# K's transform in an S4 convolution mixed with a gated unit: split as 64 by 32 points instead of 32 by 64

## The chip, the cores and the metric

The kernel runs on one core of one Trainium2 chip. The metric is the device time of one execution in microseconds, the median of several runs.

## The reference

From u (2048 x 512) the reference computes a long convolution `a` and a gated unit `b` and mixes them by a gate `g` for each row:

```
P = exp(dt * A * l)                       # 512 channels, 128 states, 2048 steps
K = einsum("dn,dnl,dn->dl", C, P, dB).real    # the kernel K, one row of 2048 for each channel
a = irfft(rfft(pad(u)) * rfft(pad(K)))[:2048] + u * Dskip
b = (sigmoid(u @ w_gate) * (u @ w_up)) @ w_down     # 512 -> 1792 -> 512
g = sigmoid(sum(u * gate_w))
out = g * a + (1 - g) * b
```

## The kernel before

All data are fp32. The three products of the gated unit use a split of every operand into two fp32r parts and three matmuls; the convolution uses plain fp32 matmuls, of which each call shows as two MATMUL rows in the trace.

**The gated unit** runs in two halves of 1024 rows, each in two blocks of 512 rows and 14 blocks of 128 hidden columns in groups of 3, 4, 4 and 3. `hidden` (L871) makes `gups` (L894), `post` makes sigmoid times up and splits it (L911 to L918), `down` makes `dps` (L946), and `add` adds it to `acc` (L962, L966). The split weights are written to DRAM (`wsp`) in the first half and read back in the second.

**The convolution** is a transform of 2048 points with a frequency shifted by a quarter, split in two stages. Of u, 64 points go first: `rows` (L531) makes `ups` (L556) for each of 16 row tiles and stores it to `a_u`. Of K, 16 groups of 32 channels are built one after the other: `preludes`, `bases` and `tables` make exponentials and sines on ScalarE and tables T (32 powers of the 64-step) and B (64 powers of the step) on VectorE; 64 calls in tiles of 128 rows by 32 columns multiply them to `kps` (L476), which `first` (L485) evicts to `kst`: a channel's 2048 values lie as 32 partitions by 64. `first` then does K's first stage: 32 points across the partitions, for two channels at a time with a block-diagonal weight `wk`, 32 calls in 64x64 tiles with 64 columns, into two banks `wps` (L503). Four evictions (L515) put them in `kev`, and every second group goes to DRAM (`a_k`, L519).

**`passes`** (L585) runs when u is done and a half of the channels (256 wide, `WIDTHS`) has its K. For each half j it takes eight steps p. A step loads u's second-stage weights `wwu` (L601) and two pieces of `a_u` (`au`, L606), and for r = 0, 1 K's second-stage weights `wwk` (L615, 128 KB each) and a piece of `a_k` (`ak`, L618), then the inverse weights `wwv` (L622). `ustep` makes `s2u`: 16 calls in 64x32 tiles, 256 columns (L639), and evicts it to `uf`. `kstep` runs once for each r: four calls in 128x64 tiles, 256 columns, into one bank `s2k` (L664), and on VectorE two products with `uf` (L673, L674) and two sums (L679, L680) for the complex product. `inverse` makes `ips` (L700) in four banks, evicts it to `ev` (L709) and stores it to `b_s`. `finals` and `last` read `b_s` back (`b_in`, L736), make `fps` (L748) and mix it into `acc` or `al`.

**Order.** The kernel is straight-line code. A planner (`Plan`, L128) takes the strands (generators) above and emits, at each moment, the step whose start plus a bias is smallest, by costs written beside each step; `BIAS`, `CHANGE`, `PACE`, `SLACK` and `EARLY` (L51 to L60) are its constants. It holds buffer slots (`slots`) and PSUM banks: three for `gups`, one for `dps` (both for `dps` at the end), and four, `XB`, for all the convolution's matmuls. All loads and stores go out in one order on SyncE's queue. K's products, sums and all the gated unit's elementwise work share VectorE and ScalarE.

## Time and profile before

| | |
|---|---|
| median of 3 runs | 648.77 us (648.64 to 650.41) |
| the profiled execution | 648.06 us, span 646.3 us |
| busy, share of the span | TensorE 98%, VectorE 86%, ScalarE 58% |
| granted TensorE clock | 1.000 |
| DMA | 133.93 MB, 207 GB/s over the span |

The profile counts time from the first instruction. "PE" is a matmul and "PEld" a weight load; a matmul's end is modelled, so its row includes a latency after the last column. A row of a group gives count, busy time and mean duration of one, then the idle time before it and what ended it. "SPq" rows are issues of transfers on SyncE's queue.

### The profile page before, as it was taken

What the parts mean: (1) busy time and instruction counts of PE and PEld (TensorE: products, weight loads), DVE (VectorE), ACT (ScalarE), POOL (GpSimd) and SP (SyncE); (2) the same over time, 40 slices, a digit from 0 to 9 for tenths busy, and PEclk for the clock granted to TensorE, in tenths of its full rate; (3) what the DMA queues carried; (4) which work ended last, traced back from release to release, by engine and by line L of the source; (5) the groups of instructions that cost most, each with busy time, mean ns of one, the idle gap of its engine ahead of it and who ended that gap; (6) DMA issues with size and microseconds to landing.
All of it is one profiled execution on the core that took longest, in us unless ns stands there. A gap on an engine that the chain in (4) does not pass through costs nothing.

```text
span 646.3 us, 15757 instructions
## 1 busy us (share of the span) xinstructions
PE 631.1 (98%) x6560; PEld 468.3 (72%) x6560; DVE 555.8 (86%) x953; ACT 374.3 (58%) x584; POOL 0.2 (0%) x4
## 2 busy tenths in 40 slices
PE   4999999999999999999999999999999999999996
PEld 3777777777787778877766787867787776666664
DVE  6859999999999999999999999999999836546515
ACT  5788787857677666576566857564676221333210
POOL 0000000000000000000000000000000000000000
PEclk9999999999999999999999999999999999999999
DMA  7974763745574446569158674542195688798377
GB/s 225 385 243 176 235 195 102 285 143 199 200 294 131 180 164 227 178 236 349 29 186 261 222 263 150 177 132 74 38 337 185 213 268 261 203 301 244 86 247 265
DMA packets 79622, 133.93 MB, mean 207 GB/s; under 512 B 7104, under 2 KB 53056, under 8 KB 74944
## 3 DMA queue, kind: packets, MB, share of 16 engines
q1 hardware_dynamic: 79552, 132.94, 62.5%
q8 instruction: 51, 0.84, 0.5%
q14 instruction: 19, 0.16, 0.1%
HBM read 79.43 MB, written 53.48 MB: 206 GB/s over the span
## 4 chain that ended last, share of the span: by engine, by line
PE 78%; DVE 14%; ACT 3%; issue 2%; DMA 1%; DVEq 0%; SPq 0%
PE gups L894 39%; PE dps L946 20%; PE kps L476 5%; PE s2k L664 4%; PE wps L503 2%; PE ips L700 2%; PE ups L556 2%; PE s2u L639 2%; PE fps L748 2%; DVE T L424 1%; DVE T L423 1%; DVE ex L395 1%; DVE t L422 1%; DVE sg L913 1%; DVE acc L966 1%
## 5 line engine op out<-in xcount | busy, mean ns | idle before, releaser
L894 PE MATMUL gups<-x,gu 128*128 128x512 f32 x1344 | 329.9, 395 | 9.2 <-ACT x L815 6.4
L894 PEld LDWEIGHTS gups<-x,gu 128*128 128x128 f32 x1344 | 251.6, 189 | 74.7 <-issue 10.0
L946 PE MATMUL dps<-dnw,h 128*128 128x512 f32 x672 | 177.5, 400 | 0.5 <-DVE h L918 0.2
L946 PEld LDWEIGHTS dps<-dnw,h 128*128 128x128 f32 x672 | 121.6, 188 | 42.7 <-issue 12.0
L917 ACT ACTIVATE h<-sg 128x512 fp32r<-128x512 f32 x56 | 35.1, 628 | 76.6 <-DVE sg L913 76.3
L673 DVE TENSOR_TENSOR tt<-s2k,uf 128x512 f32<-128x512 f32 x32 | 22.0, 688 | 31.7 <-PE s2k L664 30.7
L913 DVE TENSOR_TENSOR sg<-gups,sg 128x512 f32<-128x512 f32 x56 | 38.4, 686 | 11.5 <-PE gups L894 6.1
L515 ACT ACTIVATE kev<-wps 128x256 f32<-128x256 f32 x64 | 33.1, 672 | 25.3 <-PE wps L503 25.3
L422 DVE TENSOR_TENSOR t<-T,bz 128x64 f32<-128x64 f32 (+4 forms) x80 | 46.0, 575 | 1.0
L424 DVE TENSOR_TENSOR T<-T,t 128x64 f32<-128x64 f32 (+4 forms) x80 | 46.2, 577 | 0.7
L423 DVE TENSOR_TENSOR T<-T,bz 128x64 f32<-128x64 f32 (+4 forms) x80 | 46.0, 575 | 0.0
L966 DVE SCALAR_TENSOR_TENSOR acc<-dps,omg,acc 128x512 f32<-128x512 f32 x48 | 35.8, 747 | 10.4 <-PE dps L946 10.2
L918 DVE TENSOR_TENSOR h<-sg,h 128x512 fp32r<-128x512 f32 x56 | 38.5, 687 | 5.1 <-ACT h L917 4.9
L709 ACT ACTIVATE ev<-ips 128x256 f32<-128x256 f32 x64 | 19.8, 388 | 35.6 <-PE ips L700 32.8
L911 ACT ACTIVATE sg<-gups 128x512 f32<-128x512 f32 x56 | 33.5, 599 | 8.1 <-PE gups L894 7.9
L451 DVE TENSOR_TENSOR B<-ep 128x1024 f32<-128x1024 f32 x32 | 37.9, 1218 | 0.0
L476 PEld LDWEIGHTS kps<-B,T 128*32 128x32 f32 x2048 | 29.6, 110 | 6.8 <-issue 4.0
L394 ACT ACTIVATE af<-ex 128x1216 int32<-128x1216 f32 x16 | 19.6, 1222 | 25.3 <-DVE ex L385 25.3
L476 PE MATMUL kps<-B,T 128*32 128x64 f32 x2048 | 32.2, 220 | 0.6 <-DVE T L424 0.2
L664 PE MATMUL s2k<-ak,wwk 128*64 128x256 f32 x256 | 31.4, 386 | 0.0
L911 ACT ACT_TABLE_LOAD x23 | 29.5, 1283 | 0.4
L398 ACT ACTIVATE af<-ex 128x1216 f32<-128x1216 f32 x16 | 19.6, 1225 | 17.3 <-DVE ex L395 17.3
(79 smaller groups left out, 657.7 us busy)
## 6 DMA issues: line engine op xcount, KB each, us to landing
wsp<-gu SPq DMA_DIRECT2D x14, 1024.0 KB, 4.8
gu<-wsp SPq DMA_DIRECT2D x14, 1024.0 KB, 5.2
a_u<-evu SPq DMA_DIRECT2D x32, 256.0 KB, 3.7
a_k<-kev SPq DMA_DIRECT2D x8, 1024.0 KB, 4.8
au<-a_u SPq DMA_DIRECT2D x32, 256.0 KB, 4.4
ak<-a_k SPq DMA_DIRECT2D x32, 256.0 KB, 4.4
b_s<-ev SPq DMA_DIRECT2D x32, 256.0 KB, 4.2
b_in<-b_s SPq DMA_DIRECT2D x32, 256.0 KB, 3.5
```

The source lines that it names most:

```text
L422: yield "DVE", dve(n), lambda: V.tensor_tensor(t2, src, sb, op=OP.mult), [t, slot.t]
L423: t = yield "DVE", dve(n), lambda: V.tensor_tensor(dst, src, br, op=OP.mult), [t]
L424: t = yield "DVE", dve(n), lambda: V.tensor_tensor(dst, dst, t2[:, :, ::-1], op=OP.add), [t]
L451: tm = yield "DVE", dve(1024), lambda: V.tensor_tensor(B[:, d, 0].rearrange("p d (a b) -> p d a b", b=8), ep[:, d, 0:8, None].to_broadcast ...
L476: mm(p[32 * jj:32 * jj + 32, s], T[:, ch, c], B[:, ch, c], start=(c == 0), stop=(c == 1), tile_position=(0, 32 * jj), skip_group_check=True)
L664: mm(p2[64 * kb_:64 * kb_ + 64, c], wwk[:, kb_, 64 * c:64 * c + 64], ak[:, :, kb_], start=True, stop=True, tile_position=(0, 64 * kb_), sk ...
L894: mm(p, gu[:, a, k, dc], x[:, b, dc], start=(dc + n == 0), stop=(dc == NC - 1 and n == 2))
L911: t = yield "ACT", ("sig", act(512)), lambda: A.activation(sg, pg_, AF.Sigmoid), [tg, ss.t]
L913: t = yield "DVE", dve(512), lambda: V.tensor_tensor(sg, pu, sg, op=OP.mult), [t, tu]
L918: t = yield "DVE", dve(512), lambda: V.tensor_tensor(h[:, 1], sg, h[:, 0].bitcast(F32), op=OP.subtract), [t]
L946: mm(p, h[:, a, 128 * s:128 * s + 128], dn[:, b], start=(f == f0 and n == 0), stop=(f == f0 + gn - 1 and n == 2))
L966: te = yield "DVE", dve(512) + 0.06, lambda: V.scalar_tensor_tensor(accs[t], p, omg[:, t:t + 1], accs[t], op0=OP.mult, op1=OP.add), [tp, b ...
```

## The change

K's 2048 points are split like u's: 64 points in the first stage, 32 in the second. In `first`, the 64 calls are in 32x32 tiles (32 partitions of one channel, 32 of its 64 values) with 128 columns of the weights; the two halves h of the 64 values' index are accumulated in PSUM, into four banks in place of two. `wk` is 128 KB in place of 64 KB. `a_k` is laid out as [frequency][16 channels], so that a load of `ak` reads pieces of 64 values in place of 128, and its channels lie in another order: the matmul reads them by a view (`v`) with four levels. The second stage uses the weights `wwu` of u: `wwk` and its 32 loads go. `kstep` runs once for each p, with the 16 calls of `ustep`, into two banks, and then makes the products and sums for r = 0 and r = 1 in turn. `au`, `ak`, `uf` and `b_in` are single tiles of double width with half the slots. The planner's constants are new.

```diff
@@ -48,26 +48,19 @@
-BIAS = dict(ustep=0.15, inv=0.29, x=-4.3, w=-6.82, split=0.39, rows=-0.24, dn=0.48, urest=1.97, bases=0.29, tables=0.29,
-            first=0.19, hidden=0.81, post=0.21, down=0.68, add=0.14, passes=0.06, step=0.35, finals=0.62, last=0.45, const=2.37,
-            steps=-4.83, preludes=0.34, pw=-2.74)
-CHANGE = dict(ACT=0.77, PE=2.53)
+BIAS = dict(ustep=-0.01, inv=0.08, x=-3.86, w=-6.55, split=0.39, rows=-0.17, dn=0.13, urest=0.79, bases=0.3, tables=0.31,
+            first=0.19, hidden=0.76, post=0.18, down=0.75, add=0.36, passes=-0.59, step=0.19, finals=0.72, last=-0.01,
+            const=1.41, steps=-4.2, preludes=0.23, pw=-2.77)
+CHANGE = dict(ACT=0.8, PE=1.88)
-PACE = [4.21, 15.45]
+PACE = [2.83, 15.3]
-EARLY = -0.06
+EARLY = -0.11
...
@@ -76,6 +69,7 @@
+    wk = np.tile(fwd.reshape(P, 2, 32).transpose(2, 1, 0).reshape(32, 2 * P), (4, 1))
...
@@ -245,7 +232,7 @@
     a_u = dr.tile([2, 32, 2, 32, D], F32, name="a_u")
-    a_k = [dr.tile([w // 64, P, 32, 64], F32, name=f"a_k{j}") for j, w in enumerate(WIDTHS)]
+    a_k = [dr.tile([w // 64, P, P, 16], F32, name=f"a_k{j}") for j, w in enumerate(WIDTHS)]
     b_s = [dr.tile([32, 2, 64, w], F32, name=f"b_s{j}") for j, w in enumerate(WIDTHS)]
...
@@ -319,7 +306,7 @@
         ("pg", 1, [P, 6, QW]), ("pp", 1, [P, 2, 2, QW]), ("bz", 1, [P, 3, 5, 32]), ("ex", 1, [P, 32, 2, NA]), ("ep", 1, [P, 32, NP]),
-        ("ta", 1, [P, 32, 2, 32]), ("tb", 1, [P, 32, 2, 64]), ("t2", 2, [P, 32 * NA]), ("kst", 1, [P, 8, 64]), ("kev", 1, [P, 32, 64])))
+        ("ta", 1, [P, 32, 2, 32]), ("tb", 1, [P, 32, 2, 64]), ("t2", 2, [P, 32 * NA]), ("kst", 1, [P, 8, 64]), ("kev", 1, [P, P, 16])))
     base = [[Ev(), None] for _ in range(NG)]
...
@@ -492,28 +479,27 @@
         yield near(t)
-        banks = yield XB, 2
-        ph = [b.tile("wps") for b in banks]
+        banks = yield XB, 4
+        ph = [b.tile("wps", [P, 2, P]) for b in banks]
 
         def mms():
-            for s in range(8):
-                for jh in range(2):
-                    r = slice(64 * jh, 64 * jh + 64)
-                    for c in range(2):
-                        mm(ph[jh][64 * c:64 * c + 64, 64 * s:64 * s + 64], kst[r, s], wk[r, c], start=True, stop=True,
-                           tile_position=(64 * jh, 64 * c), skip_group_check=True)
-        t = yield "PE", ("64x64", 1.0, 128.3), mms, [t, E["wk"].t] + [b.t for b in banks]
+            for s in range(2):
+                for h in range(2):
+                    for x in range(4):
+                        for jj in range(4):
+                            r = slice(32 * jj, 32 * jj + 32)
+                            mm(ph[jj][32 * x:32 * x + 32, s], kst[r, 4 * s + x, 32 * h:32 * h + 32], wk[r, h], start=(h == 0), stop=(h == 1),
+                               tile_position=(32 * jj, 32 * x), skip_group_check=True)
+        t = yield "PE", ("32x32", 1.0, 257), mms, [t, E["wk"].t] + [b.t for b in banks]
         ks.free(t)
         if gi % 2 == 0:
             kv, = yield KEV, 1
             kevs[gi // 2] = kv, kv.tile("kev")
         kv, kev = kevs[gi // 2]
-        for jh in range(2):
-            o = 32 * (gi % 2) + 16 * jh
-            dst = kev[:, :, o:o + 16].rearrange("p k (j s) -> p s j k", j=2)
-            src = ph[jh].rearrange("p (s j k) -> p s j k", s=8, j=2)
-            te = yield "ACT", 0.95, lambda: [A.activation(dst[:, :, i], src[:, :, i], AF.Copy) for i in range(2)], [t, kv.t]
-            banks[jh].free(te)
+        for jj in range(4):
+            o = 8 * (gi % 2) + 2 * jj
+            te = yield "ACT", 0.475, lambda: A.activation(kev[:, :, o:o + 2].rearrange("p k s -> p s k"), ph[jj], AF.Copy), [t, kv.t]
+            banks[jj].free(te)
         if gi % 2 == 1:
...
@@ -589,8 +575,8 @@
         W = max(WIDTHS)
-        for n, k, s in (("wwu", 1, [P, 4, 2, 32]), ("wwv", 1, [P, 2, 2, 64]), ("wwk", 2, [P, 2, P]), ("big", 4, [P, 2 * W]),
-                        ("uf", 2, [P, 2, W]), ("t", 1, [P, 2, W]), ("ev", 1, [P, 4, W]), ("al", 2, [P, W])):
+        for n, k, s in (("wwu", 1, [P, 4, 2, 32]), ("wwv", 1, [P, 2, 2, 64]), ("big", 2, [P, 4 * W]),
+                        ("uf", 1, [P, 2, 2, W]), ("t", 1, [P, 2, W]), ("ev", 1, [P, 4, W]), ("al", 2, [P, W])):
             fin[n] = slots(fp, n, k, s)
...
@@ -600,34 +586,31 @@
                 src = a_u[:, :, :, 4 * p:4 * p + 4, OFF[j]:OFF[j + 1]].rearrange("r l c g d -> (r l c) g d")
-                s2 = yield fin["big"], 2
-                au = [s.tile("au", [P, 2, w]) for s in s2]
+                sa, = yield fin["big"], 1
+                au = sa.tile("au", [P, 4, w])
                 for i in range(2):
-                    ta.append((yield "SP", kb(w), lambda: S.dma_start(au[i], src[:, 2 * i:2 * i + 2]), [s2[i].t, E["rows"].t]))
+                    ta.append((yield "SP", kb(w), lambda: S.dma_start(au[:, 2 * i:2 * i + 2], src[:, 2 * i:2 * i + 2]), [sa.t, E["rows"].t]))
                 both = [Ev(), Ev()]
                 ready = [Ev(), None]
-                plan.spawn(ustep(j, wus, wwu, s2, au, ready, max(ta)), BIAS["ustep"])
-                res = []
+                plan.spawn(ustep(j, wus, wwu, sa, au, ready, max(ta)), BIAS["ustep"])
+                sk, = yield fin["big"], 1
+                ak = sk.tile("ak", [P, w // 16, 4, 16])
+                src = a_k[j].rearrange("o (x l) (c p r g) d -> p r (l c) (o x) g d", x=4, c=2, p=8, r=2)[p]
+                tk = []
                 for r in range(2):
-                    q = 2 * p + r
-                    wks, = yield fin["wwk"], 1
-                    wwk = wks.tile("wwk")
-                    tw = yield "SP", kb(128), lambda: S.dma_start(wwk, c_wwk[q].rearrange("p (a b) -> p a b", a=2)), [wks.t]
-                    sk, = yield fin["big"], 1
-                    ak = sk.tile("ak", [P, w // 64, 2, 64])
-                    tk = yield "SP", kb(w), lambda: S.dma_start(ak, a_k[j][:, :, 2 * q:2 * q + 2].rearrange("h r k d -> r h k d")), [sk.t, kdone[j].t]
-                    plan.spawn(kstep(j, r, wks, wwk, sk, ak, ready, both, max(tw, tk)), BIAS["step"])
+                    tk.append((yield "SP", kb(w), lambda: S.dma_start(ak[64 * r:64 * r + 64], src[r]), [sk.t, kdone[j].t]))
+                plan.spawn(kstep(j, wus, wwu, sk, ak, ready, both, max(tk)), BIAS["step"])
                 wvs, = yield fin["wwv"], 1
                 wwv = wvs.tile("wwv")
                 tv = yield "SP", kb(128), lambda: S.dma_start(wwv, c_wwv[p].rearrange("p (r c l) -> p r c l", r=2, c=2)), [wvs.t]
                 plan.spawn(inverse(j, p, wvs, wwv, ready, both, tv), BIAS["inv"])
             plan.spawn(finals(j), BIAS["finals"])
 
-    def ustep(j, wus, wwu, s2, au, ready, ta):
+    def ustep(j, wus, wwu, sa, au, ready, ta):
         w = WIDTHS[j]
-        ufs = yield fin["uf"], 2
-        uf = [s.tile("uf", [P, 2, w]) for s in ufs]
-        yield near(ta, ufs[0].t, ufs[1].t)
+        ufs, = yield fin["uf"], 1
+        uf = ufs.tile("uf", [P, 2, 2, w])
+        yield near(ta, ufs.t)
         banks = yield XB, 2
...
@@ -636,51 +619,52 @@
                         rows_ = slice(64 * r, 64 * r + 64)
-                        mm(pu[r][32 * g_:32 * g_ + 32, c], wwu[rows_, g_, c], au[g_ // 2][rows_, g_ % 2], start=True, stop=True,
+                        mm(pu[r][32 * g_:32 * g_ + 32, c], wwu[rows_, g_, c], au[rows_, g_], start=True, stop=True,
                            tile_position=(64 * r, 32 * g_), skip_group_check=True)
         t = yield "PE", ("64x32", 3.6e-3 * w, 65), mms, [ta] + [b.t for b in banks]
-        wus.free(t)
-        for s in s2:
-            s.free(t)
-        tu = []
+        sa.free(t)
         for r in range(2):
-            tu.append((yield "ACT", act(2 * w), lambda: A.activation(uf[r], pu[r], AF.Copy), [t, ufs[r].t]))
-            banks[r].free(tu[r])
+            tu = yield "ACT", act(2 * w), lambda: A.activation(uf[:, r], pu[r], AF.Copy), [t, ufs.t]
+            banks[r].free(tu)
         ready[1] = ufs, uf, tu
-        ready[0].set(tu[1])
-
-    def kstep(j, r, wks, wwk, sk, ak, ready, both, tk):
+        ready[0].set(tu)
+
+    def kstep(j, wus, wwu, sk, ak, ready, both, tk):
         w = WIDTHS[j]
         yield ready[0]
         ufs, uf, tu = ready[1]
-        uf = uf[r]
         yield near(tk)
-        bank, = yield XB, 1
-        p2 = bank.tile("s2k", [P, 2, w])
+        banks = yield XB, 2
+        pk = [b.tile("s2k", [P, 2, w]) for b in banks]
+        v = ak.rearrange("p (o x) g k -> p g o k x", x=4)
 
         def mms():
             for c in range(2):
-                for kb_ in range(2):
-                    mm(p2[64 * kb_:64 * kb_ + 64, c], wwk[:, kb_, 64 * c:64 * c + 64], ak[:, :, kb_], start=True, stop=True,
-                       tile_position=(0, 64 * kb_), skip_group_check=True)
-        t = yield "PE", ("128x64", 3.45e-3 * w, 16.4), mms, [tk, bank.t]
+                for g_ in range(4):
+                    for r in range(2):
+                        rows_ = slice(64 * r, 64 * r + 64)
+                        mm(pk[r][32 * g_:32 * g_ + 32, c], wwu[rows_, g_, c], v[rows_, g_], start=True, stop=True,
+                           tile_position=(64 * r, 32 * g_), skip_group_check=True)
+        t = yield "PE", ("64x32", 3.6e-3 * w, 65), mms, [tk] + [b.t for b in banks]
         sk.free(t)
-        wks.free(t)
-        ts, = yield fin["t"], 1
-        tt = ts.tile("tt", [P, 2, w])
-
-        def mul():
-            V.tensor_tensor(tt, p2, uf, op=OP.mult)
-            V.tensor_tensor(uf, p2[:, ::-1], uf, op=OP.mult)
-        t = yield "DVE", 2 * dve(2 * w), mul, [t, tu[r], ts.t]
-        bank.free(t)
-
-        def comb():
-            V.tensor_tensor(uf[:, 1], uf[:, 0], uf[:, 1], op=OP.add)
-            V.tensor_tensor(uf[:, 0], tt[:, 0], tt[:, 1], op=OP.subtract)
-        t = yield "DVE", 2 * dve(w), comb, [t]
-        ts.free(t)
-        both[r].set(t)
+        wus.free(t)
+        for r in range(2):
+            ts, = yield fin["t"], 1
+            tt = ts.tile("tt", [P, 2, w])
+            y = uf[:, r]
+
+            def mul():
+                V.tensor_tensor(tt, pk[r], y, op=OP.mult)
+                V.tensor_tensor(y, pk[r][:, ::-1], y, op=OP.mult)
+            te = yield "DVE", 2 * dve(2 * w), mul, [t, tu, ts.t]
+            banks[r].free(te)
+
+            def comb():
+                V.tensor_tensor(y[:, 1], y[:, 0], y[:, 1], op=OP.add)
+                V.tensor_tensor(y[:, 0], tt[:, 0], tt[:, 1], op=OP.subtract)
+            te = yield "DVE", 2 * dve(w), comb, [te]
+            ts.free(te)
+            both[r].set(te)
 
...
@@ -697,12 +681,11 @@
-                        mm(pi[g_][64 * r:64 * r + 64], wwv[rows_, r, c], uf[r][rows_, c], start=(c == 0), stop=(c == 1),
+                        mm(pi[g_][64 * r:64 * r + 64], wwv[rows_, r, c], uf[rows_, r, c], start=(c == 0), stop=(c == 1),
-        for s in ufs:
-            s.free(t)
+        ufs.free(t)
...
@@ -978,7 +960,7 @@
-                      (rows(), "rows"), (const("wk", wk, c_wk, kb(64)), "const"),
+                      (rows(), "rows"), (const("wk", wk, c_wk, kb(128)), "const"),
...
```

More of the change, by code (lines that the diff above doesn't have):

```diff
@@ L232, in run, with body @@
             self.step(st, end)
-def body(ctx, tc, xp, xt, prm, ldt, dsk, gw, wgu, wdn, c_wu, c_wf, c_wk, c_wwu, c_wwv, c_wwk, c_pw, out):
+def body(ctx, tc, xp, xt, prm, ldt, dsk, gw, wgu, wdn, c_wu, c_wf, c_wk, c_wwu, c_wwv, c_pw, out):
     nc = tc.nc
@@ L283, in steps @@
     def steps():
-        st = erl.tile([16, 10, 32], F32, name="steps")
+        st = erl.tile([16, 9, 32], F32, name="steps")
         x, nf, r, e, h1, h2 = (st[:, i] for i in range(6))
-        n, pn, b1, b2 = (st[:, i].bitcast(I32) for i in range(6, 10))
+        n, pn, b = (st[:, i].bitcast(I32) for i in range(6, 9))
         t = yield "SP", kb(2), lambda: S.dma_start(x, ldt), []
@@ L305, in scale @@
                 V.tensor_scalar(pn, nf, s, None, op0=OP.mult)
-                h, b = (h1, b1) if s < 1 else (h2, b2)
+                h = h1 if s < 1 else h2
                 V.tensor_copy(h, pn)
@@ L730, in finals @@
             w = WIDTHS[j]
-            s2 = yield fin["big"], 2
-            b = [s.tile("b_in", [P, 2, w]) for s in s2]
+            sb, = yield fin["big"], 1
+            b = sb.tile("b_in", [P, 2, 2, w])
             tb = []
```

31 lines of the change are left out of this document (8 added, 23 removed).

## Prediction

> **What bounds the kernel now.** I read the page's busy times first, then its chain of waits, then the groups by line, and last the timeline of TensorE in one stretch of the early part and one of the end.
>
> ```profile
> span 646.3 us, 15757 instructions
> PE 631.1 (98%) x6560; PEld 468.3 (72%) x6560; DVE 555.8 (86%) x953; ACT 374.3 (58%) x584; POOL 0.2 (0%) x4
> PE 78%; DVE 14%; ACT 3%; issue 2%; DMA 1%; DVEq 0%; SPq 0%
> ```
>
> TensorE is busy for 98% of the span, and 78% of the chain that ended last is its work. A busy PE row alone would prove little, since ends of matmuls are modelled; but the chain agrees. So the first question is how much TensorE time the change adds or takes. The second is whether something else stands right behind TensorE. The windows answer that:
>
> ```profile
> 440.00:460.00 20.00, 19.97 (x147) 14.46 (x147) 19.79 (x34) 11.65 (x17) 0.00 (x0) 1.00 0.28 86
> 560.00:580.00 20.00, 20.00 (x233) 12.93 (x213) 11.26 (x20) 5.79 (x15) 0.00 (x0) 1.00 0.90 273
> L503 PE MATMUL wps<-wk,kst x1024: 218/218/267, 73.5 to 517.9; 64*64 64x64 f32 x171
> L664 PE MATMUL s2k<-ak,wwk x256: 379/379/430, 300.3 to 601.1; 128*64 128x256 f32 x128
> ```
>
> The columns of the windows are PE, PEld, DVE, ACT, POOL, clock, DMA share and GB/s; the last two rows are those of single tiles, with first and last start. There are two regimes. While K's 16 groups are built (the last first-stage transform, wps, starts at 517.9) VectorE is as full as TensorE, 19.79 of 20 us. After that VectorE is half empty, TensorE stays full and the DMA engines carry a share of 0.90. The clock is 1.00 throughout.
>
> **Second stage of K (s2k): 32 small batches become 16.** The rows of one p in the last pass, and the groups:
>
> ```profile
> 569.69 1.09 PE L639 MATMUL s2u<-au,wwu 64*32 64x256 f32 x32
> 570.72 1.95 PE L664 MATMUL s2k<-ak,wwk 128*64 128x256 f32 x16
> L639 PE MATMUL s2u<-au,wwu 64*32 64x256 f32 x512 | 18.1, 382 | 0.1
> L664 PE MATMUL s2k<-ak,wwk 128*64 128x256 f32 x256 | 31.4, 386 | 0.0
> L503 PE MATMUL wps<-wk,kst 64*64 64x64 f32 x1024 | 19.0, 221 | 0.0
> ```
>
> Each fp32 call makes two matmuls (512 rows for 16 x 16 calls of s2u). A column costs (382 - 221) / (256 - 64) = 0.84 ns, and about 0.167 us of a matmul is latency. s2k's 16 matmuls run two at a time (two tiles of 64 columns): 8 x 256 x 0.84 ns = 1.72, plus 0.167 = 1.89, the row says 1.95. s2u's 32 run eight at a time: 4 x 0.215 + 0.167 = 1.03, the row says 1.09. After the change s2k has s2u's form exactly: 16 calls, tiles of 64 by 32, 256 columns. So it should cost 1.09 where it cost 1.95: -0.86 us, 16 times, **-13.8 us**. All of this lies on TensorE, which is full in both regimes.
>
> There is one difference from s2u: the moving operand is read with its inner four elements 256 bytes apart, because the channels of a group lie in another order in ak. No matmul of this kernel reads its moving operand so. The nearest rows are VectorE's:
>
> ```profile
> L680 DVE TENSOR_TENSOR uf<-tt 128x256 f32<-128x256 f32 x32 | 13.6, 425 | 1.1
> L673 DVE TENSOR_TENSOR tt<-s2k,uf 128x512 f32<-128x512 f32 x32 | 22.0, 688 | 31.7 <-PE s2k L664 30.7
> L407 DVE TENSOR_TENSOR bz<-ex,ep 128x320 f32<-128x320 f32 x16 | 13.1, 819 | 1.6 <-ACT ep L402 1.6
> 382.25 10.88 PE gups L894 x48
> ```
>
> Contiguous reads cost (688 - 425) / 256 = 1.03 ns an element, so 320 of them would take 491 ns. L407, whose two inputs are strided by more than 100 bytes, takes 819: about 1.02 ns more per element, 2.05 ns in all, twice the price. If a strided read halves the rate on TensorE as well, the question is the rate it is halved from. gups reads fp32r at 10.88 us / 48 / 512 = 0.44 ns a column; half of that rate is 0.89 ns, and the fp32 column already takes 0.84. So from this row the stride is hidden by the slow fp32 pass, at most 0.05 ns x 1024 columns x 16 = 0.8 us. If instead TensorE got an element only every 2.05 ns, as VectorE does, a pass would take 0.525 instead of 0.215 and s2k 4 x 0.525 + 0.167 + 0.06 = 2.33 us: +0.38 x 16 = +6.1 us against now. I take the first, since it is the same engine's reading; the second is a rival below.
>
> [...]
>
> **First stage (wps): 32 calls of 64 columns in 64x64 tiles become 64 calls of 128 columns in 32x32 tiles.**
>
> ```profile
> 73.51 1.16 PE L503 MATMUL wps<-wk,kst 64*64 64x64 f32 x64
> 68.64 1.99 PE L476 MATMUL kps<-B,T 128*32 128x64 f32 x128
> 560.03 0.15 PEld L639 LDWEIGHTS s2u<-au,wwu 64*32 64x32 f32 x8
> L639 PEld LDWEIGHTS s2u<-au,wwu 64*32 64x32 f32 x512 | 7.9, 106 | 8.4 <-ACT ev L709 5.3 <-issue 1.1
> ```
>
> Now: 16 rounds of four tiles, 64 x 0.84 = 54 ns each, 0.86 + 0.167 = 1.03; the row says 1.16, so a round costs 8 ns more than its stream. After: 128 matmuls in 8 rounds of 16 tiles, each 128 x 0.84 = 107 ns: 0.86 + 0.167 + 8 x 0.008 = 1.09, **-0.07 x 16 = -1.1 us**. This holds only if 16 pairs of weight load and matmul can be issued within 107 ns, 6.7 ns each. The fastest stretch in the trace is the row of eight loads: (150 - 106) / 7 = 6.3 ns a load, just enough. The upper bound is the dense row kps: (1.99 - 0.22) / 128 = 13.8 ns a matmul, which would make wps 128 x 13.8 ns + 0.22 = 1.99 us, +0.83 x 16 = +13.3. kps has only four tiles and is held by its stream (32 x 54 ns = 1.73), so I take the 6.3 ns.
>
> **Code.** wps goes from 1024 matmuls to 16 x 128 = 2048, s2k from 256 to 512: 1280 more, each with a load, so 2560 instructions on 13120.
>
> ```profile
> q8 instruction: 51, 0.84, 0.5%
> 337.61 1.84 PE L639 MATMUL s2u<-au,wwu 64*32 64x256 f32 x32
> ```
>
> 51 packets bring the code now, about 257 instructions each, so 10 more are needed. The one s2u above took 1.84 where its kind takes 1.09; if each new packet cost that 0.75 us it would be +7.5, if they are all hidden 0. Nearly all of the 51 pass without such a row, so I take **+1**.
>
> **VectorE, ScalarE, banks.** The products keep their shapes. VectorE gets none of the saving, and in the first regime it is full: TensorE's saving there (eight of the s2k, all wps: 6.9 + 1.1 = 8.0 us) can only be used by running more of the gated unit, and that needs VectorE.
>
> ```profile
> L918 DVE TENSOR_TENSOR h<-sg,h 128x512 fp32r<-128x512 f32 x56 | 38.5, 687 | 5.1 <-ACT h L917 4.9
> L913 DVE TENSOR_TENSOR sg<-gups,sg 128x512 f32<-128x512 f32 x56 | 38.4, 686 | 11.5 <-PE gups L894 6.1 <-ACT sg L911 5.2
> L966 DVE SCALAR_TENSOR_TENSOR acc<-dps,omg,acc 128x512 f32<-128x512 f32 x48 | 35.8, 747 | 10.4 <-PE dps L946 10.2
> L515 ACT ACTIVATE kev<-wps 128x256 f32<-128x256 f32 x64 | 33.1, 672 | 25.3 <-PE wps L503 25.3
> ```
>
> That is 112.7 us of VectorE for 2016 matmuls x 0.227 = 458 us of TensorE, 0.25 us per us. 8.0 us of it push K's end by 8.0 x 0.25 = **+2 us** (0 if the order finds the gaps, 8 if none of it can be used). The evictions stay 64 of 128x256 with strided writes; their 672 ns lie on ScalarE, 58% busy, so 0. wps now takes four banks of XB at once instead of two, so s2u, ups and ips stand behind it for some 3 us per group; while K is built no pass is urgent and gups and dps have banks of their own, so 0, and 16 x 0.3 at worst.
>
> **DMA and the SP queue.** The 32 loads of wwk go, with their issues; ak stays 32 loads of 256 KB, but in pieces of 256 bytes instead of 512.
>
> ```profile
> ak<-a_k SPq DMA_DIRECT2D x32, 256.0 KB, 4.4
> wwk<-c_wwk SPq DMA_DIRECT2D x32, 128.0 KB, 4.0
> 574.31 0.45 SPq L615 DMA_DIRECT2D wwk<-c_wwk  x1
> 576.07 0.36 SPq L618 DMA_DIRECT2D ak<-a_k  x1
> 580.23 2.12 PE L664 MATMUL s2k<-ak,wwk 128*64 128x256 f32 x15
> ```
>
> ak's second half is issued at 576.07 and lands 4.4 later, at 580.5, while s2k of the next p starts at 580.23: it is nearly late. Dropping two issues of 0.4 ahead of it brings it forward by about 0.8 us; the smaller pieces may cost about as much. I take 0, between -0.8 and +0.8 per p of the last eight: +-6 in the range only, with gups and dps as the cover.
>
> **Sum.** -13.8 - 1.1 + 1 + 2 = -11.9 us. The profiled execution took 648.06 (span 646.3), the median of the runs is 648.77, 0.7 above it. 648.06 - 11.9 = 636.2 by the profiled execution, and 0.7 more as a median: **637 us**.
>
> **Rivals.** *The stride is paid on TensorE* (slower). With 2.05 ns a column s2k costs +6.1 in place of -13.8, so the sum is +6.1 - 1.1 + 1 + 2 = +8, of which the 2 falls away as nothing is freed: +6, 655 us. It decides where s2k passes 1.95 us, that is from 1.7 ns a column on. For it: the only strided rows pay. Against: gups' rate. [...] A stride that costs just twice the fp32 column, 1.68 ns, would make s2k 1.95 and the whole about 649, no change.
>
> *Issue limits the 32x32 tiles*: +13.3 on wps eats the 13.8: 648. For it: no round of 16 tiles is in the trace, and 6.3 against 6.7 ns is close. Against: the loads' own row.
>
> *The end is paced by latency, not by TensorE*. Each p of the last pass goes s2u, eviction, s2k, two rounds of products, ips, eviction:
>
> ```profile
> 571.90 0.69 DVE L673 TENSOR_TENSOR tt<-s2k,uf 128x512 f32<-128x512 f32 x1 [3.58 <-PE s2k L664]
> 576.81 0.42 DVE L680 TENSOR_TENSOR uf<-tt 128x256 f32<-128x256 f32 x1
> 576.91 1.48 PE L700 MATMUL ips<-uf,wwv 32*64 32x256 f32 x32
> 579.21 1.09 PE L639 MATMUL s2u<-au,wwu 64*32 64x256 f32 x32
> ```
>
> From 569.69 to 579.21 is 9.5 us, and the first product starts right after the first half of s2k, as it will start after the whole of a shorter s2k: the cycle does not shrink. If the gated unit's work, which fills TensorE meanwhile, can't be moved ahead, the last eight savings (6.9) are lost: 637 + 6.9 = 644. Against: 8 x 9.5 = 76 us from 520 gives 596, and the final products after it hold filler that can go.
>
> **How the numbers follow.** A measurement of this kernel can tell about 0.3%, 2 us, from no change. Forecast 0.44, its own range 630 to 641; latency 0.16 (644); stride in full 0.23 (655), doubled 0.07 (649); issue 0.10 (648). Of the issue case 0.02 is faster, 0.03 the same, 0.05 slower; of the doubled stride 0.05 is the same, 0.02 slower. Faster: 0.44 + 0.16 + 0.02 = 0.62; same: 0.03 + 0.05 = 0.08; slower: 0.23 + 0.05 + 0.02 = 0.30. The range goes from 630 (code and VectorE at nothing, 634, and the loads bringing 4) to 655; it leaves out the far half of the stride case, where late products lengthen the cycle too, and what lies below.
>
> **What would show it.** s2k with 512 rows and a mean near 382 ns, 32 of them in about 1.1 us; a mean much above 386 is the stride. wps 128 in about 1.1 us; 2 us is the issue. The last wps near 518 to 520 says VectorE paces K; a cycle of s2u still near 9.5 us with idle TensorE says latency. The forecast is wrong if s2k takes over 1.9 us, or if TensorE's idle time grows by more than 5 us.

## The result, and the profile after

The changed kernel takes 677.48 us (median of 4 runs, 676.1 to 680.76) where the kernel before took 649.59 on the same chip: 1.043 times as long, 95% interval 1.038 to 1.048. The forecast was 637, range 630 to 655: wrong in sign and outside the range. The profiled execution took 678.57 us, its span is 676.5.

Of the page of the kernel after: its head, the code queue, the chain's shares, the groups of the two changed transforms, and the loads of ak (KB each, median us from issue to landing):

```profile
span 676.5 us, 18251 instructions
...
PE 647.9 (96%) x7840; PEld 470.7 (70%) x7840; DVE 559.4 (83%) x955; ACT 373.9 (55%) x583; POOL 0.2 (0%) x4
...
q8 instruction: 61, 1.00, 0.6%
...
PE 69%; DVE 13%; DMA 10%; ACT 4%; issue 2%; SPq 1%; DVEq 0%; ACTq 0%
...
L646 PE MATMUL s2k<-ak,wwu 64*32 64x256 f32 x512 | 35.2, 608 | 0.4 <-DMA ak<-a_k 0.3
L491 PE MATMUL wps<-wk,kst 32*32 32x128 f32 x2048 | 30.4, 278 | 0.0
...
ak<-a_k SPq DMA_DIRECT2D x32, 256.0 KB, 5.4
```

By the terms for s2k and wps TensorE should have become 14.9 us less busy (13.8 and 1.1). It became 16.8 us busier (631.1 to 647.9): s2k's group went from 31.4 to 35.2 us instead of falling to 18, wps from 19.0 to 30.4. Its idle time (span less busy) went from 15.2 to 28.6. The two increases give 16.8 + 13.4 = 30.2 us, the whole difference of the spans.

The windows of the same stretches as before:

```profile
440.00:460.00 20.00, 19.75 (x253) 14.16 (x238) 16.62 (x28) 14.89 (x19) 0.00 (x0) 1.00 0.58 187
560.00:580.00 20.00, 19.83 (x239) 12.07 (x238) 10.98 (x20) 5.62 (x14) 0.00 (x0) 1.00 0.86 225
```

The tile wps (shortest, median and longest matmul in ns, first and last start in us):

```profile
L491 PE MATMUL wps<-wk,kst x2048: 264/268/293, 78.7 to 543.9; 32*32 32x128 f32 x187
```

TensorE's timeline, one group of wps and two p of the last pass:

```profile
78.67 1.90 PE L491 MATMUL wps<-wk,kst 32*32 32x128 f32 x128
...
566.21 1.09 PE L622 MATMUL s2u<-au,wwu 64*32 64x256 f32 x32
567.10 2.79 PE L646 MATMUL s2k<-ak,wwu 64*32 64x256 f32 x32
...
576.80 1.09 PE L622 MATMUL s2u<-au,wwu 64*32 64x256 f32 x32
577.68 1.96 PE L646 MATMUL s2k<-ak,wwu 64*32 64x256 f32 x32
```

In the first window VectorE fell from 19.79 to 16.62 us (the order differs, so it need not be the same work). The last wps starts at 543.9 instead of 517.9: 26 of the 30 us are lost before K is complete; from there to the end of the span it is 132.6 us, before 128.4. The two stretches can be compared, as nearly the same work of the gated unit is done by then: 1176 matmuls of gups in both, 513 of dps, before 516. A group of wps takes 1.90 us where it took 1.16. s2k takes 1.96 us where s2u, of the same tiles and weights and as many columns, takes 1.09. Sixteen groups of 1.96 make 31.4 of its 35.2 us, no less than before. Of the other 3.8, 3.6 are stops inside five groups until the second half of ak was there (in the group of 2.79 us, a load issued at 561.2 that landed 6.6 us later). A load of ak lands after 5.4 us, not 4.4 (medians).

### The profile page after: what moved, and what is told of

The parts are those of the page before. It is cut to its first block, busy times and chain, and to the rows that moved or that the text cites. A ratio compares the mean times of both kernels' runs of the same rounds, so it can differ in the third digit from the quotient of the medians.

```text
span 676.5 us, 18251 instructions
## 1 busy us (share of the span) xinstructions
PE 647.9 (96%) x7840; PEld 470.7 (70%) x7840; DVE 559.4 (83%) x955; ACT 373.9 (55%) x583; POOL 0.2 (0%) x4
## 4 chain that ended last, share of the span: by engine, by line
PE 69%; DVE 13%; DMA 10%; ACT 4%; issue 2%; SPq 1%; DVEq 0%; ACTq 0%
PE gups L876 33%; PE dps L928 18%; PE s2k L646 5%; PE kps L463 3%; PE wps L491 3%; PE s2u L622 2%; PE ips L684 2%; DMA st<-wgu 2%; DMA out<-al 2%; DMA b_in<-b_s 1%; PE ups L542 1%; DVE B L438 1%; DMA ak<-a_k 1%; DMA u<-xp 1%; ACT L893 1%
## 5 line engine op out<-in xcount | busy, mean ns | idle before, releaser
L928 PE MATMUL dps<-dnw,h 128*128 128x512 f32 x672 | 175.4, 400 | 1.3 <-ACT acc L944 1.0
L893 ACT ACTIVATE sg<-gups 128x512 f32<-128x512 f32 x56 | 33.6, 600 | 16.1 <-PE gups L876 15.7
L646 PE MATMUL s2k<-ak,wwu 64*32 64x256 f32 x512 | 35.2, 608 | 0.4 <-DMA ak<-a_k 0.3
L491 PE MATMUL wps<-wk,kst 32*32 32x128 f32 x2048 | 30.4, 278 | 0.0
```

What stands on the lines that cost most here:

```text
L491: mm(ph[jj][32 * x:32 * x + 32, s], kst[r, 4 * s + x, 32 * h:32 * h + 32], wk[r, h], start=(h == 0), stop=(h == 1), tile_position=(32 * jj ...
L646: mm(pk[r][32 * g_:32 * g_ + 32, c], wwu[rows_, g_, c], v[rows_, g_], start=True, stop=True, tile_position=(64 * r, 32 * g_), skip_group_c ...
L893: t = yield "ACT", ("sig", act(512)), lambda: A.activation(sg, pg_, AF.Sigmoid), [tg, ss.t]
L928: mm(p, h[:, a, 128 * s:128 * s + 128], dn[:, b], start=(f == f0 and n == 0), stop=(f == f0 + gn - 1 and n == 2))
```

## The experiments

Unless said otherwise the kernel before, run beside them, took 649.2 to 649.9 us, and ratios are to it. Where one time stands, there is no interval.

**What a stride costs: e1_contig and e5_pairs.** The channels are dealt to the groups in another order (`deal`, applied to the parameters ahead of the launch), so that ak holds them in the order in which s2k wants them.

```
-        v = ak.rearrange("p (o x) g k -> p g o k x", x=4)
+        v = ak.rearrange("p q g k -> p g q k")              # e1: runs of 16 values
+        v = ak.rearrange("p q g (a b) -> p g a q b", b=2)   # e5: runs of 2 values
```

> The changed kernel, with K's channels dealt to the 16 groups in another order (on the way in, by a transposition of the parameters), so that s2k reads ak in runs of 16 neighbouring values; instructions, sizes and order are the same. If the stride is what makes s2k slow, its mean goes from 608 ns to about 382, a group of 32 from about 1.96 us to 1.09, and TensorE gets back 16 x 0.87 = 14 us: 677 becomes 661 to 665, or a little less if matmuls that come when the planner expected them also remove idle time. If s2k is slow for another reason (its weights, the loads of 256-byte pieces, its banks), the mean stays near 608 and the time near 677.

> The changed kernel with K's channels dealt so that s2k reads runs of two neighbouring values (8 bytes) and then jumps 256 bytes; only K's channel order on the way in and the view change. If what costs is a new place for each single value, and two neighbours absorb it, s2k's mean is near 382 ns, as with runs of 16. If each jump costs the 0.89 ns that the change showed for each value, half as many jumps give about 382 + 114 = 496 ns. If any view with steps is read at half rate, it stays at 608.

e1: 668.11 us (667.37 to 668.93), ratio 1.0286 [1.0265, 1.0307]: 9.4 us less than the changed kernel, and less of a gain than the 12 to 16 expected. e5: one time, 669.71. The tile s2k of e1, then of e5:

```profile
L646 PE MATMUL s2k<-ak,wwu x512: 372/376/401, 313.2 to 620.8; 64*32 64x256 f32 x171
```

```profile
L646 PE MATMUL s2k<-ak,wwu x512: 373/373/407, 313.6 to 623.2; 64*32 64x256 f32 x171
```

The median of 610 ns falls to 376 and 373 (the means are 608, 380 and 379). Without the stride s2k's matmuls cost what the forecast said; with it a column takes (608 - 167) / 256 = 1.72 ns in place of 0.84, twice as long. And a run of two values (8 bytes) is enough to be rid of it.

**What the first stage costs: e4_wide, e7_half, e9_order, e10_rounds8.** e4 holds kst with its halves outside, so that one weight takes two channels (32 by 64 tiles, 32 calls). e7 leaves out half of the columns, e9 exchanges the two inner loops, e10 comes back to a tile after 8 calls in place of 16.

```
-  mm(ph[jj][32 * x:32 * x + 32, s], kst[r, 4 * s + x, 32 * h:32 * h + 32], wk[r, h], ...)       # x in 0..3
+  mm(ph[jj][64 * x:64 * x + 64, s], kst[r, h, 4 * s + 2 * x:4 * s + 2 * x + 2]..., wk[r, h], ...)  # e4, x in 0..1
+  mm(ph[jj][32 * x:32 * x + 32, s, :64], kst[r, 4 * s + x, ...], wk[r, h, :64], ...)            # e7
+  for jj in range(4): for x in range(4):                                                        # e9
+  for xh in range(2): for s ...: for h ...: for x in (2 * xh, 2 * xh + 1):                      # e10
```

> The changed kernel with the first stage in 32x64 tiles: two channels' weights in one call (kst is written with the halves h outside the channels, so that 64 weights lie side by side), 32 calls of 128 columns in place of 64; the same results in the same banks, same order. Streaming takes the same 8 x 107 ns. If the 32x32 form is held by a price for each pair of weight load and matmul (12.9 ns measured, 16 x 12.9 = 206 ns a round), half the pairs make wps about 1.1 us in place of 1.90, 16 x 0.8 = 13 us: 661 to 665. If it is held by loads of weights (columns times pairs, the same number in both) or by the stream, wps stays near 1.9 us and the time near 677.

> The changed kernel with only the first 64 of 128 columns in the first stage (the other half of the frequencies is left out and filled with copies); still 64 calls in 32x32 tiles. The stream of a round of 16 tiles falls from 107 to 54 ns. If each pair of weight load and matmul has a price of about 12.9 ns there, a round stays at 206 ns and first to last start at 1.63 us. If a tile's next weights (102 ns) are not loaded behind its own stream, a round is 102 + 54 = 156 ns, 1.25 us in all. If it is the stream that runs at half speed with 16 tiles, 0.83 us.

> The changed kernel with the two inner loops of the first stage swapped: four column tiles of one row group in turn, then the next row group; the same calls. If the price is for each pair, nothing changes, 1.63 us from first to last start. If row groups in turn (as now) or column tiles in turn matter, because two loads into the same rows or columns follow each other, it moves by over 0.2 us either way.

> The changed kernel with the first stage's calls in another order: a tile comes back after 8 calls instead of 16, the same 64 calls in 32x32 tiles. The half-width run took 156 ns a round, 102 of load and 54 of stream, so the next weights of a tile were not loaded behind its stream. If that is because a load can't be pulled ahead over 32 instructions, a round of 8 tiles takes the stream's 107 ns, 16 rounds 1.7 us, as now. If 32x32 tiles never load behind their own stream, it is 16 x 209 ns = 3.3 us.

Times: e4 675.32 us (673.54 to 678.0), ratio 1.040 [1.0369, 1.0431]; one time each of e7 (677.77), e9 (679.31) and e10 (683.58). The first group of wps in TensorE's timeline, of e4, e7 and e9 in turn:

```profile
78.55 1.21 PE L491 MATMUL wps<-wk,kst 32*64 32x128 f32 x64
```

```profile
80.58 1.48 PE L491 MATMUL wps<-wk,kst 32*32 32x64 f32 x128
```

```profile
79.00 1.90 PE L491 MATMUL wps<-wk,kst 32*32 32x128 f32 x128
```

128 matmuls with half the columns take 1.48 us instead of 1.90, so the issue of 128 pairs is not the limit (the matmuls of the first two rounds start 6 to 7 ns apart, too). Exchanging the two inner loops changes nothing (e9, 1.90). Take off the last matmul (0.27, in e7 0.21) and eight rounds of streams (8 x 107 ns, 8 x 54 ns): 0.77 and 0.84 us stay, 96 and 105 ns a round, whatever the columns. That is one weight load, whose row in the changed kernel's tile wps is:

```profile
L491 PEld LDWEIGHTS wps<-wk,kst x2048: 101/102/106, 78.7 to 543.8; 32*32 32x32 f32 x187
```

So with 16 tiles in turn each round takes as long as stream and load one after the other. With 8 tiles it doesn't: e4's rounds take (1.21 - 0.27) / 8 = 117 ns, and e10's rounds of 8 start 110 ns apart (it has 16 of them, so its group is no shorter). e4 thus brings wps back to its old price, 11 us less of TensorE's time, and the kernel becomes 2 us faster; the intervals of the two ratios overlap, so even that is not certain. The 12 to 16 us expected of it didn't come.

**Does TensorE's time set the end: e18_half_s2k and e19_more_wps.** Both are the kernel before, in its own order. e18 makes half of s2k's matmuls, e19 repeats part of the first stage.

```
-            for c in range(2):                       # s2k, and the products read half 0 twice
+            for c in range(1):                       # e18
-            for s in range(8):                       # first stage
+            for s in list(range(8)) + list(range(6)):  # e19
```

> The kernel before, with half of s2k's matmuls left out: one of the two column halves is not computed, and the products read the other half twice. The order of all instructions stays as it is, and the operands stay contiguous; only TensorE's time falls, by 128 matmul streams: s2k 1.95 to about 1.1 us a pass, 16 x 0.85 = 13.8 us, just what the prediction took off for the changed s2k. Theory A, the prediction's premise (TensorE's saved time comes off the end, but for the 2 us that VectorE gives back): 635 to 638 us. Theory B (something else holds the end as well: VectorE while K is built, the cycle of a pass later): less than half of the 13.8 comes off, 642 to 649, the last wps stays at 515 to 518 us, and TensorE's idle time rises from 15 to 22 or more.

> The kernel before, with 12 of the 16 row-column quarters of extra work a first-stage group: wps makes 56 calls of its 64-column matmul in place of 32 (six of the eight rows are computed twice, with the same values), so that a group takes about 1.65 us on TensorE from first to last start, as it does in the changed kernel, in place of 0.94. Nothing else differs, the order least of all. That is 0.7 x 16 = 11 us more of TensorE, all of it while K is built. Theory A (TensorE's time there counts in full): 659 to 662 us and the last wps at 527 to 530. Theory B (VectorE sets the pace there, TensorE's time is taken up by idle time): 649 to 654.

e18: 648.85 us, ratio 0.9991 [0.9976, 1.0007] over 10 runs. e19: 665.73 us, ratio 1.0256 [1.0214, 1.0297]. The page of e18:

```profile
span 645.7 us, 15501 instructions
...
PE 621.8 (96%) x6432; PEld 459.4 (71%) x6432; DVE 556.4 (86%) x953; ACT 373.5 (58%) x584; POOL 0.2 (0%) x4
...
PE 57%; DVE 29%; ACT 6%; DMA 4%; issue 4%; SPq 1%; DVEq 0%; ACTq 0%
```

Its waits of VectorE for the first product's inputs (us in total, times, longest):

```profile
DVE tt L673 <- ACT uf L647: 24.2, 8, 3.9
...
DVE tt L673 <- PE s2k L664: 2.1, 1, 2.1
```

And its tile wps:

```profile
L503 PE MATMUL wps<-wk,kst x1024: 218/218/267, 74.1 to 518.8; 64*64 64x64 f32 x171
```

s2k's group fell from 31.4 to 18.0 us; TensorE lost 9.3 us of busy time and the span 0.6. K ends at 518.8, not earlier than 517.9. That fits VectorE as the pace of that part: from 80 to 480 us it is busy for 391.3 of 400, as in the kernel before. In the passes the products waited 30.7 us for s2k (row L673 of the kernel before); now they wait 24.2 for the eviction of s2u's result. Half of the transform gone, VectorE's wait mostly changed its name. The chain shows the same in one line: PE 78% became 57%, DVE 14% became 29%. What e18 can't say is whether an order chosen anew for the shorter s2k would have used the time; no run tried that.

e19, its page, then its tile wps:

```profile
span 663.4 us, 17293 instructions
...
PE 641.0 (97%) x7328; PEld 479.1 (72%) x7328; DVE 557.4 (84%) x953; ACT 373.5 (56%) x584; POOL 0.2 (0%) x4
...
L503 PE MATMUL wps<-wk,kst 64*64 64x64 f32 x1792 | 30.9, 220 | 2.8 <-issue 2.6
```

```profile
L503 PE MATMUL wps<-wk,kst x1792: 213/218/267, 73.9 to 534.5; 64*64 64x64 f32 x200
```

Here 30.9 - 19.0 = 11.9 us more of wps cost 16.1 us, and K ends 16.6 later. So the two directions are not alike in that order: time added to TensorE in wps counts in full, and somewhat more (the forecast of that case was 659 to 662), time taken from s2k counts for nothing.

**Both mends: e6_both, and the held weights: e12_wwu2, e14_wwu2_only.** e6 is e1 and e4 together. In the changed kernel wwu is kept until s2k has read it, and the next load of wwu waits for that; e12 (on e6) and e14 (on the changed kernel) put it into two buffers in turn, in the same order.

```
-                wwu = wus.tile("wwu")
+                wwu = fp.tile([P, 4, 2, 32], F32, tag=f"wwu{(8 * j + p) % 2}", name="wwu")
```

> Both mends together: runs of 16 neighbouring values for s2k, and the first stage in 32x64 tiles; order and planner constants of the changed kernel. Every matmul now costs what the planner assumed. If TensorE's work is what sets the end, as the prediction had it, the time is 636 to 640, some 10 us faster than before. If the order itself holds idle time, since VectorE paces K until the last first stage and a chain of dependent steps paces the last pass, TensorE's gain turns into idle time and it is 646 to 653, the kernel before within 1%. The two single gains, 9.4 and 2.2 us, add to 666 if they are independent; they should give more together if the second only pays once the first is mended, as matmuls then come when the order expects them.

> Both mends, and two buffers in turn for wwu (the order of every queue stays the same). In the changed kernel wwu is held until s2k is done, where before it was free after s2u; the load of the next wwu, and behind it on SyncE's queue the next au and ak, waits for that. The trace of both mends shows s2k stopped by 0.6 to 1.4 us in half of its groups, until the second half of ak lands, and 10.7 us of its lag behind the planned order arises at s2k. If the held wwu makes ak late, the stops shrink by about 1.2 us each and the time falls from 667 by 5 to 10 us. If ak is late by its 256-byte pieces and longer issues alone, or because it waits for its own buffer, the time stays within 2 us of 667.

> The changed kernel with two buffers in turn for wwu and nothing else changed. If the held wwu costs time of its own, it falls from 677 by 3 to 10 us; if the slow s2k (1.96 us) hides it, it stays within 2 us.

e6: 666.84 us, ratio 1.0277 [1.0248, 1.0306]: neither of its two cases, but the sum of the two single gains. e12: 664.14, 1.0214 [1.0191, 1.0238], between its two cases. e14: 678.12, 1.0433 [1.041, 1.0457], no gain. The page of e6, then the waits that its tile ak shows (us, times), then its tile wps:

```profile
span 664.0 us, 16203 instructions
...
PE 626.1 (94%) x6816; PEld 462.4 (70%) x6816; DVE 558.5 (84%) x955; ACT 373.2 (56%) x583; POOL 0.2 (0%) x4
...
PE 60%; DVE 17%; DMA 14%; SPq 3%; issue 3%; ACT 2%; DVEq 0%; ACTq 0%
```

```profile
  DMA ak<-a_k: 3.6, 6
```

```profile
L491 PE MATMUL wps<-wk,kst x1024: 267/268/319, 78.7 to 535.6; 32*64 32x128 f32 x171
```

TensorE has 5 us less to do than in the kernel before (626.1 to 631.1), and the span is 17.7 longer: 37.9 us idle. ak's loads stand in the chain with 6% and stop s2k six times; with the second wwu buffer that falls to 1.4 us in two stops, and 2.7 us are won (4.1 by the ratios). K still ends at 535.6, and from there to the end e6 takes 128.4 us, just as the kernel before. So all of its 17.7 us are lost while K is built, nearly all as idle time of TensorE. The windows up to the last wps, of the kernel before and then of e6 (the columns are those of the windows above), show it:

```profile
0.00:517.90 517.90, 507.88 (x5514) 386.43 (x5516) 490.99 (x836) 345.91 (x518) 0.20 (x4) 1.00 0.60 201
```

```profile
0.00:535.60 535.60, 508.80 (x5655) 383.05 (x5657) 495.05 (x844) 344.54 (x517) 0.20 (x4) 1.00 0.62 192
```

TensorE is idle there for 10.0 us before and for 26.8 in e6. ak's stops are 1.4 us of that; the rest is spread over many waits, the longest new one 2.6 us of gups for the sigmoid (L893).

**The order: e2_costs, e3_oldconst, e8_newconst, e16_after_reordered, e15_a, e15_b, e17_best.** The order of the units comes from the planner's costs and constants. e2 tells it the measured costs with the constants left as they are; e3 gives the changed kernel the old constants, e8 gives the kernel before the new ones; e16 has the measured costs and constants chosen anew. e15_a, e15_b and e17 do so for the mended kernel: e15_a and e15_b with two slots of wwu and ak's dearer loads told, e17 with one slot and without that.

```
-        t = yield "PE", ("32x32", 1.0, 257), mms, ...
+        t = yield "PE", ("32x32", 1.75, 257), mms, ...        # e2, e16
-        t = yield "PE", ("64x32", 3.6e-3 * w, 65), mms, ...
+        t = yield "PE", ("64x32", 6.9e-3 * w, 65), mms, ...   # e2, e16
```

> The changed kernel, with the planner told what the trace measured: 1.75 us for the first stage in place of 1.0, and twice the cost for s2k. No instruction changes, only the order. If the part of the loss that is not TensorE's own work (some 14 us of idle time and K's end 26 us later) comes from an order that was planned with times that were too short, it becomes 662 to 668 and TensorE's idle time falls from 28 to about 15 us. If that part comes from the loads or from the four banks, it stays within 4 us of 677.

> The changed kernel with the planner's constants of the kernel before (biases, pace, change costs); the new layout and matmuls stay. If the new constants are part of the loss, it becomes faster by over 5 us; if they are only noise beside the wrong costs, it stays within 5 us of 677 either way.

> The kernel before with the planner's constants of the changed kernel, a control on the order: no matmul changes. The changed kernel with the constants of before took 719 in place of 677. If constants fit only the kernel that they were chosen for, this one takes 670 to 700 in place of 649 too; if the new constants are good for both, it stays near 649.

> The changed kernel, matmuls and layouts unmended, with the planner told the measured costs of its first stage and of s2k, and with constants chosen anew for these costs. If an order made for costs that were too short is part of the loss of 28 us, it becomes 660 to 668. If the loss is all in the matmuls and loads, it stays at 675 to 680.

> Both mends, two buffers of wwu, the planner told the right form and cost of the first stage and ak's longer issue and landing, and constants chosen anew (started from those of the kernel before). If the remaining 14 us come from the order, it is 646 to 652, as before the change or a little under. If they come from the split itself, it stays at 660 or more.

> As e15_a, with another set of constants (started from those of the changed kernel). The same two cases: 646 to 652, or 660 and more; that two sets agree within 4 us would show that it is not one lucky order.

> Both mends, one buffer of wwu, the planner told the right form of the first stage but nothing of ak's longer issue and later landing, and constants chosen anew. If ak's loads cost nothing beyond what an order can hide, it is as fast as e15_a; if the planner must know of them, it is slower than e15_a by 3 us or more, with s2k stopped until ak lands.

| kernel | us | ratio, 95% |
|---|---|---|
| e2_costs | 716.67 | 1.1011 [1.0969, 1.1052] |
| e3_oldconst | 719.48 | 1.1068 [1.1024, 1.1112] |
| e8_newconst | 684.1 | one time |
| e16_after_reordered | 676.26 | 1.0408 [1.0388, 1.0427] |
| e15_a | 659.21 | 1.0146 [1.012, 1.0172] |
| e15_b | 663.72 | 1.0219 [1.019, 1.0247] |
| e17_best | 660.01 | 1.0173 [1.0143, 1.0202] |

Either set of constants fits its own kernel only: moved to the other they cost 34 us (e8, one time) and 42 (e3), and true costs under constants chosen for wrong ones cost 39 (e2, where a gain of 9 to 15 was one case). Part of that came with a lower granted clock, 0.983, 0.957 and 0.980 in that order. With constants chosen for it the changed kernel stays at 676 (e16): this one choice gives no sign that its loss is the order's, though it doesn't rule out a better order. For the mended kernel the order gives up to 7.6 us (e6 to e15_a, two slots of wwu included) or 6.8 (e6 to e17, one slot); e15_b's constants, 4.5 us slower than e15_a's, give nothing over e12. e17, whose planner knows nothing of ak's dearer loads, is within 0.8 us of e15_a: an order can hide them. No version of the split came below the kernel before. e15_a's page, then its tile wps:

```profile
span 655.4 us, 16147 instructions
...
PE 623.5 (95%) x6816; PEld 461.3 (70%) x6816; DVE 553.8 (85%) x953; ACT 362.6 (55%) x577; POOL 0.2 (0%) x4
```

```profile
L490 PE MATMUL wps<-wk,kst x1024: 264/268/319, 72.6 to 520.3; 32*64 32x128 f32 x171
```

K ends at 520.3, 2 us behind the kernel before, and from there it is 135 us to the end in place of 128. But that doesn't place the loss after K, since this order has left more of the gated unit for later: by then 1122 matmuls of gups and 510 of dps are done, in the kernel before 1176 and 516, about 15 us of TensorE's time (54 x 0.25 + 6 x 0.26, by the groups' busy times before). TensorE's idle time up to the last wps is 23.4 us, in the kernel before 10.0, so here too most of the added idle time falls while K is built.

## Why the prediction was wrong, step by step

**What bounds the kernel.** This step failed whatever s2k and wps cost: "All of this lies on TensorE, which is full in both regimes", so 13.8 us less of it were taken as 13.8 us less of time. e18 takes as much of s2k away (13.4 us of its group) in the order of the kernel before, and the time stays at 0.9991. A 98% busy row and a 78% share of the chain told which engine is full in this order, not what a saving on it is worth: VectorE was as full beside it while K is built (19.79 of 20 us in the window), and later the products' wait for s2k had the wait for s2u's eviction right behind it. In that order the "+2 for VectorE" should have been the whole of the 8.0 us of that regime, and the later 6.9 us were lost as in the rival on latency. That rival named the mechanism (0.16); its price, 644, still left it the first regime's gain.

**s2k, -13.8.** The step "from this row the stride is hidden by the slow fp32 pass" failed. gups' rate, 0.44 ns a column in another type, said nothing of how an fp32 pass reads: by e1 and e5 the strided column costs 1.72 ns, twice the fp32 column. That is the "doubled" case of the rival, whose price was right (s2k 1.95 us, the row says 1.96) and whose chance, 0.07, was far too small. s2k costs what it did, and 3.8 us more, nearly all in stops, so nothing was saved; the stride is worth 9.4 us of the time (e1). What the trace of the kernel before had for the stride, L407's double price on VectorE (2.05 in place of 1.03 ns an element), was set against gups' rate and given too little weight; the runs show the same factor on TensorE: with single values a matmul takes 608 ns, with two neighbours at a time 379 by e5's mean.

**wps, -1.1.** The step that took the eight loads' 6.3 ns as the price of a round failed, and so did its rival by issue, though its price was close (+13.3, measured (1.90 - 1.16) x 16 = 11.8). (With that price the rival's terms add up to 649 to 651 us, not 648.) The limit is neither issue nor stream but the weight load, which isn't hidden when 16 tiles take turns (204 ns a round, the stream 107, a load 102; in e7 159, with a stream of 54) and is with 8 (110 ns in e10, 117 in e4). The sum had hidden it because it is hidden with four and eight tiles, as in wps and s2u of the kernel before (1.16 and 1.09 us a group, stream and latency alone 1.03 in both, with loads of 134 and 106 ns). As much added to wps costs some 16 us in the order of before (e19); taken away in the changed kernel's order it gives back about 2 (e4).

**Code, +1.** Ten packets more were forecast, and 61 stand in place of 51. What they cost can't be parted from the rest. e19, with 1536 instructions more and its order unchanged, has two waits "issue" ahead of wps, 2.6 us in all, where the kernel before has none.

**VectorE, ScalarE, banks, 0.** The 64 evictions keep their time (median 666 ns, before 680). What wps' claim on four banks costs was not tried by itself, since taking it away changes the order. In the trace of the changed kernel one matmul of fps waits for such an eviction, 0.7 us.

**Loads, 0 ± 6.** They got dearer: 5.4 in place of 4.4 us to landing, and they stop s2k for 3.6 us in the changed kernel (above) and for as much in e6. The wait on wwu, which the prediction didn't name, costs 2.7 us in the mended kernel (e6 to e12) and nothing in the changed kernel (e14); that the slow s2k hides it there fits, but was not tried by itself.

**How it adds up, and what stays open.** Two adverse cases that the prediction held apart, stride and first stage, came together, and the gain they were set against didn't come in any run. e19 and e1 give 16 and 9 us, near the 28 measured, but in different orders; undoing both in the changed kernel's order gives back only 10.6 us, so they can't simply be added. A lower granted clock is not what makes the changed kernel slow: e16 takes 676.26 at 0.999. That a mended kernel with less TensorE work stands 10 to 17 us above the kernel before is not settled. Shown are the held weights (2.7) and the order (up to 7.6, the slots included). For the last 10, ak's smaller pieces, the four banks and an order less well fitted remain, untried apart. The traces narrow it: in e15_a no matmul waits for ak or for an eviction of wps, while gups waits 5.4 us for its weights in the first 26 us, long before K's first transform (72.6). The mean granted clock of e15_a is 0.989, before 1.000, which is at most 0.011 x 655.4 = 7.2 us of TensorE's time, an estimate. This points at the order, but no run shows it.

**The signs it had named** were right for s2k: a mean "much above 386 is the stride" (608), and the forecast wrong if s2k takes over 1.9 us (1.96) or TensorE's idle time grows by more than 5 (13.4). The one for wps, "2 us is the issue", would have misled: 1.90 came, from the weight loads.

## What to carry to other kernels

A full engine is worth its saving only if what waits right behind it is saved too: for each gain ask which wait ends last once it is taken, and let a second full engine in the same window cap it. Price an access pattern by the element type and the engine that does it; without such a row, take the factor that the trace shows elsewhere (L407 on VectorE, 1.03 to 2.05 ns an element) on the rate of the matmul in question as the likeliest case, not a side case (0.84 to 1.72 ns a column came). In a kernel with an order fixed ahead, time above what the order was made for can be paid in full (e19), and taking that away gains (e1, 12.1 us less of TensorE's busy time, 9.4 us), while time saved below it can be worth nothing (e18); so the range should lean to the slow side.

## What the runs showed of the hardware

- A single-value stride on the moving operand doubles an fp32 matmul's column (0.84 to 1.72 ns, the changed kernel); runs of two values are free (e5, mean 379 ns at 256 columns; runs of 16, e1: 380).
- With 16 tiles of 32 by 32 in turn, each call with a new weight, a round takes stream plus load (about 204 ns at 128 columns in the changed kernel, 159 at 64 in e7); with 8 tiles little more than the stream of 107 (at 128 columns 110 ns in e10, 117 in e4).
- A 256 KB load in 256-byte pieces to 64 partitions (ak, the changed kernel) holds the SP queue 633 ns (median) in place of 432 and lands after 5.4 us in place of 4.4, against one in 512-byte pieces to 128 partitions (the kernel before); the two differences were not parted.
